# The shared product of the first spectral layer: added on VectorE, or copied by ScalarE into the bank that TensorE then adds onto

## The chip, the cores and the metric

The kernel runs on one core of one Trainium2 chip. The metric is the device time of one execution in microseconds (us). TensorE (PE) multiplies, with its weight loads shown apart as PEld; VectorE (DVE) and ScalarE (ACT) do the elementwise work; GpSimd (POOL) does a little of it; the DMA queues are fed mostly by SyncE (SP). PSUM, where the products land, has eight banks of 512 fp32 values in each of 128 partitions.

## The reference, cut to what matters

```
Xf = rfft2(x)                                   # x: [2, 1, 4096, 640], over the 4096 positions
z  = Xf in 4 blocks of 160 channels;  zr, zi
hr = relu(zr @ w1[0] - zi @ w1[1] + b1[0])      # layer 1, per block
hi = relu(zi @ w1[0] + zr @ w1[1] + b1[1])
or_ = hr @ w2[0] - hi @ w2[1] + b2[0]           # layer 2
oi_ = hi @ w2[0] + hr @ w2[1] + b2[1]
a  = irfft2(softshrink(or_) + 1j * softshrink(oi_))
b  = (gelu(x @ w_gate) * (x @ w_up)) @ w_down
out = sigmoid(sum(x * gate_w)) * a + (1 - gate) * b
```

The change lies in the first two lines of `h`. The two complex sums hold one product in common: with s = zr + zi, each of hr and hi is a product of s with one matrix, plus a product of one part of z with another matrix. The kernel works out three products in place of four.

## The kernel before, in words

All products run as pairs of fp32r parts: an operand is split into a rounded high part, written by ScalarE (`high`, L285), and the rest, written by VectorE or GpSimd (`low`, L288). A product is then three matmuls, high by high, high by low and low by high (`mms`, L305 to L307).

The kernel has three stretches. To about 1360 us run the gate and up projections and the first step of the forward transform. From about 1360 to 1760 us run the two spectral layers. After that run the last step of the inverse transform and the down projection.

The spectral stretch is a list of 64 steps (b, c, n): two batch entries, eight chunks of 256 frequencies, four blocks of channels. Chunk (0, 0) is wider by two columns ("wide") and takes a path of its own; it is steps 4 to 7. The program order of each engine is the order in which the Python code issues instructions, and each engine keeps to it. One pass i of the loop over the steps issues:

- in some passes `rest`, the second transform step for the channels that the blocks leave over: a transform on TensorE, then `high` and `low` of `zz`. It stands ahead of layer 1;
- `main_z` for step i+1: eight matmul records of the transform (`fwd2`, L993), then on ScalarE the high part `z` and a copy `zt` (L1005), on VectorE the low part of `z` and the sum `zt` (L1008). What is left, the split of `zs` (that is s), is returned as a function `sums`;
- `mlp1` for step i: the shared product `pk` (3 matmuls on `zs`); `kc`, its copy to SBUF by ScalarE (L1096); two groups of 5 matmuls, one for each half of the bank `pm`; two VectorE additions of `kc` onto them, `hs` (L1103); `sums()`; `relu_split` of `hs` into `h` (ScalarE L1056, VectorE L1057); then the 32 channels left over, `last` (5 matmuls, L1079 to L1081), with a ScalarE copy (L1109) and a VectorE sum (L1110);
- `mlp2` for step i-1: two times 8 matmuls on `h`, each followed by a ScalarE activation `m` (L1138) and a VectorE instruction `y` (L1139);
- `more()`: two ScalarE activations `hl` (L1113, L1114) and one VectorE instruction (L1115) for step i;
- where i is odd, `inv1` for the pair that ended at step i-2: 12 matmuls, two copies `is` on ScalarE (L1174) and two on VectorE (L1176);
- where i is even, `y_split` for the pair that ended at step i-1: two `high` of `ys` on ScalarE, one `low` on VectorE and one on GpSimd.

So ScalarE's queue at the start of a pass holds, for odd i, the two `ys` of the pass before, then `zz` if there is a `rest`, then `z`, `zt` and `kc`. For even i it holds the two `is` instead of `ys`.

The banks of PSUM come from one pool of eight. A bank goes back when the last instruction that reads it is through.

Of the kernel before, what the change touches and what calls it, by code (L numbers as in the profile page):

```python
# [12 lines left out]
AF = mybir.ActivationFunctionType  # L13
OP = mybir.AluOpType

P = 128
# [6 lines left out]
CH = 256  # L23
# [198 lines left out]
def spectral_mix_kernel(ctx: ExitStack, tc: tile.TileContext, a):  # L222
    nc = tc.nc
# [11 lines left out]
    def bank():  # L235
        return psum.tile([P, 512], F32, name="bank", tag="bank")
# [6 lines left out]
    def mid(shape, dt=F32, name="mid"):  # L243
        if not gap:
            gap.extend([tiny([P, 1], name="gap"), pool.tile([P, 112], F32, name="gap", tag="gap", bufs=1)])
            for t in gap:
                nc.gpsimd.memset(t, 0.0)
        return pool.tile(shape, dt, name=name, tag="mid", bufs=14)

    def small(shape, dt=F32, name="small"):  # L250
        return pool.tile(shape, dt, name=name, tag="small", bufs=18)

    def tiny(shape, dt=F32, name="tiny"):
        return pool.tile(shape, dt, name=name, tag="tiny", bufs=15)
# [7 lines left out]
    def flush():  # L262
        for dst, src in late:
            ld(dst, src)
        late.clear()
# [12 lines left out]
    b1r = consts.tile([64, NBLK], F32, name="b1r")  # L278
# [16 lines left out]
    def by_two(m):  # L295
        return m.rearrange("p (k i) -> p i k", k=2)

    def mm3(dst, pairs):

        ops = []  # L300
        for (lh, ll), (rh, rl) in pairs:
            ops += [(lh, rh)] + ([(ll, rh)] if ll is not None else []) + [(lh, rl)]
        mms(dst, ops)

    def mms(dst, ops):  # L305
        for i, (l, r) in enumerate(ops):
            nc.tensor.matmul(dst, l, by_two(r), start=i == 0, stop=i == len(ops) - 1)  # L307

# [622 lines left out]
    wide = lambda b, c: (b, c) == (0, 0)  # L933
# [6 lines left out]
    def two(b, c, name):  # L940

        if wide(b, c):
            return [mid([P, 2, CW], F32R, name=name) for h in range(2)]
        t = mid([P, 2, 2, CH], F32R, name=name)
        return [t[:, h] for h in range(2)]
# [3 lines left out]
    def part_of(b, c, k):  # L949

        if not wide(b, c):
            return tiny([P, CH], name=("zt", "kc", "hs")[k])
        if not WT:
            WT.append(mid([P, 3, CW], name="wt"))
        return WT[0][:, k]
# [28 lines left out]
    def sc_pop(b, c):  # L984
        for b_, kp in [(b, kp) for kp in range(4)] + ([(1, 0)] if wide(b, c) else []):
            SC.pop((b_, c, kp))
# [53 lines left out]
    def main_z(b, c, n):  # L1040
        F = width(b, c)
        z = two(b, c, "z")
        if wide(b, c):
            zs = small([P, 2, F], F32R, name="zs")
            zs = [zs[:, h] for h in range(2)]
        else:
            if chunks.index((b, c)) < 2 * NCH - 4:
                zs = mid([P, 2, F], F32R, name="zs")
                zs = [zs[:, h] for h in range(2)]
            else:  # L1050
                zs = [tiny([P, F], F32R, name="zs") for h in range(2)]
        Z[b, c, n] = z, zs
        return fwd2(b, c, P * n, z, zs)

    def relu_split(dh, dl, src):
        nc.scalar.activation(dh, src, AF.Relu)  # L1056
        nc.vector.scalar_tensor_tensor(dl, src, 0.0, dh.bitcast(F32), op0=OP.max, op1=OP.subtract)  # L1057

    def mlp1(b, c, n, sums):
        F = width(b, c)  # L1060
        z, (sh, sl) = Z.pop((b, c, n))
        w, wl = W1[n], W1L[n]
        t1, t2 = ZL1[b, c], ZL2[b, c]

        part = lambda k: (w[:, k:k + P], w[:, LOW1 + k:LOW1 + k + P])
        wl = wl.rearrange("p h c -> p (h c)")


        def group(dst, m):
            r = 1 - m  # L1070
            wh, wlo = part(OUT1[m])
            mms(dst, [(wh, z[0][:, r]), (wh, z[1][:, r]), (wlo, z[0][:, r]),
                      (wl[:, P * m:P * m + P], t1[:, n, :F]), (wl[:t2.shape[0], 384 + P * m:512 + P * m], t2[:, n, :F])])

        def last(dst):

            for r in range(2):
                k = LAST1[r]
                nc.tensor.matmul(dst, w[:, k:k + P], by_two(z[0][:, r, :F]), start=r == 0, stop=False, skip_group_check=True)  # L1079
                nc.tensor.matmul(dst, w[:, k:k + P], by_two(z[1][:, r, :F]), start=False, stop=False, skip_group_check=True)  # L1080
            nc.tensor.matmul(dst, wl[:, 256:384], by_two(t1[:, n, :F]), start=False, stop=True, skip_group_check=True)  # L1081
        h = two(b, c, "h")
        if wide(b, c):
            if n < 2:
                x = small([P, 2, CW], F32R, name="hl")
                nc.gpsimd.memset(x[64:66, 1].bitcast(F32), 1.0)
                HW[n] = x[:, 0], x[:66, 1]
            hA, hB = HW[n % 2]
        else:
            hA, hB = hl1[n % 2], hl2[n % 2]  # L1090
        H[b, c, n] = (h, hA, hB)
        pk = bank()
        wh, wlo = part(OUT1["k"])
        mms(pk[:, :F], [(wh, sh[:, :F]), (wh, sl[:, :F]), (wlo, sh[:, :F])])
        kc, hs = part_of(b, c, 1), (small if wide(b, c) else mid)([P, 2, F], name="hs")
        nc.scalar.activation(kc[:, :F], pk[:, :F], AF.Copy)  # L1096
        pm = [bank()] * 2 if F == CH else [bank(), bank()]
        for r in range(2):
            d = pm[r][:, r * CH:(r + 1) * CH] if F == CH else pm[r][:, :F]
            group(d, r)  # L1100
        for r in range(2):
            d = pm[r][:, r * CH:(r + 1) * CH] if F == CH else pm[r][:, :F]
            nc.vector.tensor_add(hs[:, r, :F], d, kc[:, :F])  # L1103
        sums()
        relu_split(h[0], h[1], hs)
        pl = bank()
        last(pl[:, :F])
        hs = part_of(b, c, 2)[:64]
        nc.scalar.activation(hs, pl[64:, :F], AF.Copy)  # L1109
        nc.vector.scalar_tensor_tensor(hs, pl[:64, :F], b1r[:, n:n + 1], hs, op0=OP.add, op1=OP.add)  # L1110

        def rest_of():
            nc.scalar.activation(hB[:64, :F], hs, AF.Relu)  # L1113
            nc.scalar.activation(hA[:64, :F], hs, AF.Relu)  # L1114
            nc.vector.scalar_tensor_tensor(hA[64:, :F], hs, 0.0, hB[:64, :F].bitcast(F32), op0=OP.max,  # L1115
                                           op1=OP.subtract)
        return rest_of
# [229 lines left out]
    def h_s4(i):  # L1347
        d = HR[i]
        for k in range(2):
            nc.vector.tensor_sub(d["s2"][k], d["a12"][k], d["s2"][k])  # L1350
        d["s4"] = d.pop("s2")
# [163 lines left out]
    last = len(keys) - 1  # L1515
# [59 lines left out]
    for k, (b, n2) in enumerate(a_seq):  # L1575
        i, j = steps_a[k]
# [16 lines left out]
    for i, (gr, tp) in enumerate(keys):  # L1593
        if deep((gr, tp)) and tp % 2:
            p, f = x_deep(gr, tp)
# [9 lines left out]
    for k, (l, pb) in enumerate(((1, 0), (1, 1), (2, 0), (2, 1))):  # L1605
        s0 = (5, 12, 19, 26)[k]
        f = prep(l, pb)
# [15 lines left out]
    for i, key in enumerate(keys):  # L1623
# [18 lines left out]
        for j, t in enumerate(quads):  # L1642
# [10 lines left out]
            n = len(late)  # L1653
# [18 lines left out]
    steps = [(b, c, n) for b, c in chunks for n in range(NBLK)]  # L1672
    S = len(steps)
    steps[S - 6:S - 2] = [(1, NCH - 1, 0), (1, NCH - 1, 1), (1, NCH - 2, 2), (1, NCH - 2, 3)]
    uu, ahead = {}, {}
    todo = {}
    for ch in range(1, 2 * NCH):
        b, c = chunks[ch]
# [6 lines left out]
    def events(i, j):  # L1685
        for f, *args in todo.get((i, j), []):
            f(*args)
    wl = lambda part, *js: [(wd_load, j, part) for j in js]
# [13 lines left out]
    for i in range(S + 2):  # L1702
        events(i, 0)
        flush()
        if i < S:
            events(i, 1)
            if i + 1 < S:
                sums = main_z(*steps[i + 1]) if i else ahead_z
                if steps[i + 1][2] == 3:
                    sc_pop(*steps[i + 1][:2])  # L1710
            more = mlp1(*steps[i], sums if i + 1 < S else lambda: None)
        if 0 <= i - 1 < S:
            mlp2(*steps[i - 1])
        if i < S:
            more()
        if 0 <= i - 2 < S and steps[i - 2][2] % 2:
            inv1(steps[i - 2][0], steps[i - 2][1], steps[i - 2][2] // 2)
            if wide(*steps[i - 2][:2]) and steps[i - 2][2] == 3:
                HW.clear()
                WT.clear()  # L1720
        if 0 <= i - 1 < S:
            b, c, n = steps[i - 1]
            if n % 2:
                y_split(b, c, n // 2)
            if i == S:
                uu.update(inv2(0))
        for f, *args in fin.get(i, []):
            f(*args)


    SEQ = dict(enumerate(("s3", "s4", "a12", "a22", "s1")))
    DUO = {0: "s1", 2: "s3", 3: "a12", 4: "s4"}
    for i in range(len(c_seq)):
        n = i + 1 if i + 1 < len(c_seq) else None
# [3 lines left out]
        def step(k):  # L1738
            def f():
# [7 lines left out]
                if k == (1 if i else 0):  # L1747
                    h_s4(i)
                op = (SEQ if i == 0 else DUO).get(k)
                if op:  # L1750
# [44 lines left out]
```

## Time and profile before

| | |
|---|---|
| median of 3 runs | 2466.82 us (2465.4 to 2467.61) |
| the profiled execution | 2466.74 us |
| its span, first to last instruction | 2465.0 us |
| PE busy | 2445.0 us, 20239 matmuls |
| DVE busy | 2065.8 us |
| ACT busy | 1486.9 us |
| POOL busy | 390.5 us |
| granted TensorE clock | 1.0 |
| DMA | 499.50 MB, 203 GB/s |

The busy time of an engine is the sum of its instructions' times, overlaps counted once. In a timeline each row is one instruction or a few alike in a row: start, time, engine, line, operation, out<-in, shapes, count, and in square brackets how long the engine had been idle before and what ended that. Matmuls are pipelined, so the rows of PE overlap: the start of the next row says more than the time of one.

### The profile page before, as it was taken

The page shows a single profiled execution, that of the slowest core. Times are in us where ns is not written, and L with a number is a line of the kernel's source. Part 1 is how long each engine was busy: PE and PEld are TensorE (multiplying, and loading weights), DVE is VectorE, ACT ScalarE, POOL GpSimd, SP SyncE. Part 2 cuts the span into 40 slices and gives each one's busy share as a digit, 9 for nine tenths or more (in the row PEclk, how much of TensorE's full clock was granted, in tenths as well). Part 3 has the DMA queues.
Part 4 walks back from the last instruction along what each step waited for, and adds up shares of the span by engine and source line. Part 5 has one row for each costly group of instructions (what it writes and reads, how often), then busy time and mean ns, then how long its engine had stood idle before and what let it go on. Part 6 is the DMA issues. An engine that isn't in the chain of part 4 may idle for free.

```text
span 2465.0 us, 54653 instructions
## 1 busy us (share of the span) xinstructions
PE 2445.0 (99%) x20239; PEld 2430.0 (99%) x20239; DVE 2065.8 (84%) x4323; ACT 1486.9 (60%) x3503; POOL 390.5 (16%) x404
## 2 busy tenths in 40 slices
PE   9999999999999999999999999999999999999999
PEld 9999999999999999999999999999999999999999
DVE  7777788777777877877767888888899999999998
ACT  5555556666666666666556788888744454455443
POOL 0111100000000000000003111111043334333342
PEclk9999999999999999999999999999999999999999
DMA  6666667777778687777677446467854444544443
GB/s 208 212 229 214 242 208 232 224 263 236 250 236 261 196 257 250 237 227 248 222 234 234 148 139 174 147 173 244 308 176 145 140 150 156 167 161 153 148 145 112
DMA packets 351422, 499.50 MB, mean 203 GB/s; under 512 B 26028, under 2 KB 223276, under 8 KB 351156
## 3 DMA queue, kind: packets, MB, share of 16 engines
q1 hardware_dynamic: 333684, 445.02, 56.1%
q0 software_dynamic: 17472, 51.00, 5.7%
q8 instruction: 159, 2.61, 0.4%
q14 instruction: 107, 0.88, 0.1%
HBM read 307.10 MB, written 188.81 MB: 201 GB/s over the span
## 4 chain that ended last, share of the span: by engine, by line
PE 71%; DVE 19%; issue 5%; DMA 3%; ACT 2%; SPq 0%; DVEq 0%; ACTq 0%
PE bank L572 48%; PE bank L307 11%; DVE ho L288 7%; PE bank L1421 6%; DVE s2s L288 3%; PE bank L993 3%; DVE uu L1426 2%; PE bank L704 2%; DVE uu L1389 1%; PE bank L827 1%; DVE hs L1350 1%; DMA s<-scr 1%; PE bank L1079 0%; PE bank L1080 0%; DMA xraw<-in_xT_dram 0%
## 5 line engine op out<-in xcount | busy, mean ns | idle before, releaser
L572 PE MATMUL bank<-xo,w 128*128 128x256 f32 x11196 | 1298.3, 275 | 3.1 <-ACT u L598 1.5
L572 PEld LDWEIGHTS bank<-xo,w 128*128 128x128 f32 x11196 | 1276.1, 192 | 5.9 <-ACT u L598 2.1
L1421 PE MATMUL bank<-wx,ho 128*128 128x320 f32 x3844 | 532.4, 300 | 5.6 <-DVE ho L288 5.5
L1421 PEld LDWEIGHTS bank<-wx,ho 128*128 128x128 f32 x3844 | 524.4, 189 | 10.2 <-DVE ho L288 10.0
L285 ACT ACTIVATE ho<-hraw 128x640 fp32r<-128x640 f32 x320 | 168.3, 574 | 118.5 <-PE bank L1421 83.7
L288 DVE TENSOR_TENSOR ho<-hraw,ho 128x640 fp32r<-128x640 f32 (+3 forms) x384 | 226.8, 632 | 6.4 <-ACT ho L285 3.4
L598 ACT ACTIVATE u<-bank 128x256 f32<-128x256 f32 x328 | 125.4, 382 | 161.2 <-PE bank L572 154.7
L288 DVE TENSOR_TENSOR xs<-xr,xs 64x640 fp32r<-64x640 f32 x128 | 105.0, 820 | 75.9 <-ACT xs L285 73.4
L650 DVE TENSOR_TENSOR u<-bank,u 128x256 f32<-128x256 f32 x204 | 85.9, 421 | 79.8 <-ACT u L598 78.7
L288 DVE TENSOR_TENSOR xo<-xraw,xo 128x512 fp32r<-128x512 f32 x194 | 133.3, 688 | 17.0 <-ACT xo L285 15.7
L307 PE MATMUL bank<-wm,h 128*128 128x320 f32 (+1 forms) x792 | 129.7, 300 | 0.5 <-DVE h L1057 0.4
L829 DVE TENSOR_TENSOR as<-bank,as 64x320 f32<-64x320 f32 x256 | 113.9, 484 | 18.3 <-ACT as L828 16.4
L285 ACT ACTIVATE xo<-xraw 128x512 fp32r<-128x512 f32 x194 | 121.7, 627 | 8.4 <-DMA xraw<-in_xT_dram 7.3
L598 ACT ACTIVATE p<-bank 128x256 f32<-128x256 f32 x144 | 55.3, 384 | 104.6 <-DVE h L661 57.7
L288 DVE TENSOR_TENSOR s2s<-s,s2s 128x320 fp32r<-128x320 f32 x128 | 115.7, 963 | 2.4 <-ACT s2s L285 1.5
L307 PEld LDWEIGHTS bank<-wm,h 128*128 128x128 f32 (+1 forms) x792 | 111.8, 186 | 2.1 <-DVE h L1057 0.6
L572 PE MATMUL bank<-wx,ho 128*128 128x320 f32 x764 | 110.4, 300 | 0.9 <-DVE ho L288 0.9
L285 ACT ACTIVATE xs<-xr 64x640 fp32r<-64x640 f32 x128 | 93.9, 734 | 28.2 <-DMA xr<-in_x_dram 26.4
L828 ACT ACTIVATE as<-bank 64x320 f32<-64x320 f32 x256 | 96.9, 427 | 20.3 <-PE bank L827 15.4
L572 PEld LDWEIGHTS bank<-wx,ho 128*128 128x128 f32 x764 | 105.7, 189 | 2.1 <-DVE ho L288 2.1
L780 POOL MEMSET h<- 64x512 f32 x16 | 8.3, 522 | 614.2 <-DVE h L665 178.2
L599 ACT ACTIVATE h<-bank 128x256 f32<-128x256 f32 x204 | 77.8, 381 | 29.4 <-PE bank L572 27.8
(196 smaller groups left out, 3892.8 us busy)
## 6 DMA issues: line engine op xcount, KB each, us to landing
xo<-xD SPq DMA_DIRECT2D x124, 512.0 KB
xraw<-in_xT_dram SPq DMA_DIRECT2D x215, 256.0 KB
hD<-h SPq DMA_DIRECT2D x184, 256.0 KB
hraw<-hD SPq DMA_DIRECT2D x128, 320.0 KB
xD<-xo POOLq DMA_DIRECT2D x64, 512.0 KB, 3.6
sc<-scr SPq DMA_DIRECT2D x65, 320.0 KB
xr<-in_x_dram SPq DMA_DIRECT2D x64, 320.0 KB
scr<-as SPq DMA_DIRECT2D x64, 320.0 KB
```

The costliest lines, as they stand in the source:

```text
L285: nc.scalar.activation(dst, src, AF.Copy, scale=scale)
L288: eng.tensor_sub(dst, src, hi.bitcast(F32))
L307: nc.tensor.matmul(dst, l, by_two(r), start=i == 0, stop=i == len(ops) - 1)
L572: nc.tensor.matmul(dst, l, by_two(r), start=first and i == 0, stop=i == len(ops) - 1, skip_group_check=True)
L598: copy = lambda d, s_: nc.scalar.activation(d, s_, AF.Copy)
L599: gelu = lambda d, s_: nc.scalar.activation(d, s_, AF.Gelu_apprx_tanh)
L650: nc.vector.tensor_add(u4, C, u4)
L704: nc.tensor.matmul(acc, l, by_two(r), start=first and i == 0, stop=i == 2, skip_group_check=True)
L828: nc.scalar.activation(stg[hi, cs], pa[lo, :320], AF.Copy)
L829: nc.vector.tensor_add(stg[hi, cs], pa[hi, :320], stg[hi, cs])
L993: nc.tensor.matmul(pz.rearrange("p (r e k f) -> p k r e f", r=2, e=2, k=4)[:, kp], SC[b, c, kp][:, o:o + P], ft.rearrange("p (r e f) -> p ...
L1421: nc.tensor.matmul((X, Y)[k], l, by_two(r), start=n[k] == 0 and not (more and k), stop=n[k] == tot[k] - 1, skip_group_check=True)
```

## The change: what it does, and the diff

For all steps but the wide ones:

- Two PSUM banks are taken at the first step and kept to the end of the stretch (`seeds`). They are used in turn. Each is written once at the start by a matmul over all its 512 columns with `start=True`.
- `pk` comes first in the step. ScalarE then copies it, read twice over, into both halves of the step's bank `d`: one instruction with 512 output columns into PSUM, in place of `kc` with 256 into SBUF.
- Behind that come `main_z` of step i+1 (`ahead()`), then `last`, then the two groups of 5 matmuls, now with `start=False`: they add onto what ScalarE wrote.
- The two VectorE additions `hs` are gone. `relu_split` reads the bank itself.
- `rest_sum`, the copy and sum for `last`, stands ahead of `sums()` and `relu_split`.

In the wide steps only the place of `ahead()` changes: it comes behind `pk`.

```
-    def mms(dst, ops):
+    def mms(dst, ops, first=True):
         for i, (l, r) in enumerate(ops):
-            nc.tensor.matmul(dst, l, by_two(r), start=i == 0, stop=i == len(ops) - 1)
+            nc.tensor.matmul(dst, l, by_two(r), start=first and i == 0, stop=i == len(ops) - 1, skip_group_check=not first)
...
+    seeds = []
+
-    def mlp1(b, c, n, sums):
+    def mlp1(b, c, n, ahead):
...
-                      (wl[:, P * m:P * m + P], t1[:, n, :F]), (wl[:t2.shape[0], 384 + P * m:512 + P * m], t2[:, n, :F])])
+                      (wl[:, P * m:P * m + P], t1[:, n, :F]), (wl[:t2.shape[0], 384 + P * m:512 + P * m], t2[:, n, :F])],
+                F > CH)
...
+        def rest_sum(pl):
+            hs = part_of(b, c, 2)[:64]
+            nc.scalar.activation(hs, pl[64:, :F], AF.Copy)
+            nc.vector.scalar_tensor_tensor(hs, pl[:64, :F], b1r[:, n:n + 1], hs, op0=OP.add, op1=OP.add)
+            return hs
...
-        kc, hs = part_of(b, c, 1), (small if wide(b, c) else mid)([P, 2, F], name="hs")
-        nc.scalar.activation(kc[:, :F], pk[:, :F], AF.Copy)
-        pm = [bank()] * 2 if F == CH else [bank(), bank()]
-        for r in range(2):
-            d = pm[r][:, r * CH:(r + 1) * CH] if F == CH else pm[r][:, :F]
-            group(d, r)
-        for r in range(2):
-            d = pm[r][:, r * CH:(r + 1) * CH] if F == CH else pm[r][:, :F]
-            nc.vector.tensor_add(hs[:, r, :F], d, kc[:, :F])
-        sums()
-        relu_split(h[0], h[1], hs)
-        pl = bank()
-        last(pl[:, :F])
-        hs = part_of(b, c, 2)[:64]
-        nc.scalar.activation(hs, pl[64:, :F], AF.Copy)
-        nc.vector.scalar_tensor_tensor(hs, pl[:64, :F], b1r[:, n:n + 1], hs, op0=OP.add, op1=OP.add)
+        if F == CH:
+            if not seeds:
+                seeds.extend(bank() for k in range(2))
+                for d in seeds:
+                    nc.tensor.matmul(d, wl[:, :P], t1[:, :2], start=True, stop=True)
+            pm = seeds.pop(0)
+            seeds.append(pm)
+            d = pm.rearrange("p (r f) -> p r f", r=2)
+            nc.scalar.activation(d, pk[:, None, :F].broadcast_to((P, 2, F)), AF.Copy)
+            sums = ahead()
+            pl = bank()
+            last(pl[:, :F])
+            for r in range(2):
+                group(d[:, r], r)
+            hs = rest_sum(pl)
+            sums()
+            relu_split(h[0], h[1], d)
+        else:
+            sums = ahead()
...
-            if i + 1 < S:
+            def following(i=i):
+                if i + 1 == S:
+                    return lambda: None
                 sums = main_z(*steps[i + 1]) if i else ahead_z
                 if steps[i + 1][2] == 3:
                     sc_pop(*steps[i + 1][:2])
-            more = mlp1(*steps[i], sums if i + 1 < S else lambda: None)
+                return sums
+            more = mlp1(*steps[i], following)
```

More of the change, by code (lines that the diff above doesn't have):

```diff
@@ L1094, in mlp1 @@
         mms(pk[:, :F], [(wh, sh[:, :F]), (wh, sl[:, :F]), (wlo, sh[:, :F])])
-        kc, hs = part_of(b, c, 1), (small if wide(b, c) else mid)([P, 2, F], name="hs")
-        nc.scalar.activation(kc[:, :F], pk[:, :F], AF.Copy)
-        pm = [bank()] * 2 if F == CH else [bank(), bank()]
-        for r in range(2):
-            d = pm[r][:, r * CH:(r + 1) * CH] if F == CH else pm[r][:, :F]
-            group(d, r)
-        for r in range(2):
-            d = pm[r][:, r * CH:(r + 1) * CH] if F == CH else pm[r][:, :F]
-            nc.vector.tensor_add(hs[:, r, :F], d, kc[:, :F])
-        sums()
-        relu_split(h[0], h[1], hs)
-        pl = bank()
-        last(pl[:, :F])
-        hs = part_of(b, c, 2)[:64]
-        nc.scalar.activation(hs, pl[64:, :F], AF.Copy)
-        nc.vector.scalar_tensor_tensor(hs, pl[:64, :F], b1r[:, n:n + 1], hs, op0=OP.add, op1=OP.add)
+        if F == CH:
[17 more added lines that the diff above has]
+            sums = ahead()
+            kc, hs = part_of(b, c, 1), small([P, 2, F], name="hs")
+            nc.scalar.activation(kc[:, :F], pk[:, :F], AF.Copy)
+            pm = [bank(), bank()]
+            for r in range(2):
+                group(pm[r][:, :F], r)
+            for r in range(2):
+                nc.vector.tensor_add(hs[:, r, :F], pm[r][:, :F], kc[:, :F])
+            sums()
+            relu_split(h[0], h[1], hs)
+            pl = bank()
+            last(pl[:, :F])
+            hs = rest_sum(pl)
         def rest_of():
@@ L1728, in spectral_mix_kernel @@
             f(*args)
+    seeds.clear()
     SEQ = dict(enumerate(("s3", "s4", "a12", "a22", "s1")))
```

## The prediction, on record before the changed kernel ran

> **What bounds the kernel now.** I read the page first, then the busy time by stretches, the waits of the spectral stretch, and its timeline, TensorE and ScalarE apart.
>
> ```profile
> span 2465.0 us, 54653 instructions
> ...
> PE 2445.0 (99%) x20239; PEld 2430.0 (99%) x20239; DVE 2065.8 (84%) x4323; ACT 1486.9 (60%) x3503; POOL 390.5 (16%) x404
> ```
>
> TensorE is busy for all but 20 us. An edit gains only where TensorE idles, or where it takes work from TensorE; it loses wherever it makes TensorE wait. The change keeps every matmul, so the second question is where TensorE idles in the stretch it touches.
>
> ```profile
> core 0: us, PE busy (x) PEld busy (x) DVE busy (x) ACT busy (x) POOL busy (x), PEclk, DMA share, GB/s
> 1412.00:1717.00 305.00, 305.00 (x2478) 303.58 (x2478) 263.36 (x577) 247.97 (x598) 38.01 (x25) 1.00 0.59 175
> 1717.00:1760.00 43.00, 41.20 (x321) 40.02 (x320) 35.60 (x77) 32.89 (x79) 5.24 (x5) 1.00 0.73 241
> 1760.00:1800.00 40.00, 36.71 (x262) 35.45 (x261) 37.39 (x69) 24.68 (x55) 9.70 (x8) 1.00 0.82 311
> ```
>
> In the steady part (steps 8 to 56) TensorE idles for 0.00 of 305 us at full clock. Only the last steps and what follows them show idle time, 1.8 and 3.3 us. VectorE (86% busy) and ScalarE (81%) are close behind, and where ScalarE idles it waits for VectorE:
>
> ```profile
> ACT zs L285 <- DVE zt L1008: 39.5, 47, 0.9
> ...
> ACT h L1056 <- DVE hs L1103: 11.2, 49, 0.3
> ```
>
> These 51 us are slack of ScalarE that TensorE never feels. The change spends it, and the point is where in the step it spends it.
>
> **Removed and lengthened work.** Grouped rows of the same window:
>
> ```profile
> L1103 DVE TENSOR_TENSOR hs<-bank,kc 128x256 f32<-128x256 f32 x98 | 36.6, 415 | 0.0
> ...
> L285 ACT ACTIVATE ys<-y 128x640 fp32r<-128x640 f32 x48 | 32.6, 730 | 0.0
> L1056 ACT ACTIVATE h<-hs 128x512 fp32r<-128x512 f32 x49 | 30.9, 631 | 11.2 <-DVE hs L1103 11.2
> L285 ACT ACTIVATE z<-bank 128x512 fp32r<-128x512 f32 x49 | 28.8, 587 | 0.3 <-PE bank L993 0.3
> ...
> L1096 ACT ACTIVATE kc<-bank 128x256 f32<-128x256 f32 x49 | 18.6, 380 | 0.0
> ...
> L285 ACT ACTIVATE zz<-bank 128x512 fp32r<-128x512 f32 x13 | 7.6, 581 | 0.0
> ```
>
> VectorE loses two `hs` a step, 36.6 us in these 49 steps. TensorE waits for nothing of VectorE's here (0.00 idle), so this counts nothing. ScalarE's copy grows from 256 columns into SBUF to 512 into PSUM. No row writes PSUM from ScalarE. The bounds are 0.38 us (`kc`, as if the second half were free) and 0.73 us (`ys`, more columns, SBUF on both sides). I take 0.59, from `z`: PSUM source and as many columns. The Trainium skill ("ScalarE: Activation LUTs", "Step-by-step: what each stage is for") says that PSUM is the lower-latency destination for ScalarE. If that were worth what the source's side shows here, 0.631 against 0.587 or 0.044 us, the sum below would be about 1.2 us smaller. No row here shows it. `relu_split` reading PSUM rather than SBUF differs by the same 0.04 us and is on no path of TensorE. The two first matmuls into the kept banks, 512 columns each, are once 0.4 us.
>
> **The added wait.** Until now nothing on TensorE waited for `kc`; only VectorE did. Now both groups wait for ScalarE's copy, the seed. Queued behind them on TensorE are `mlp2` of the step before and, in odd passes, `inv1`; ScalarE's `m` and VectorE's `y` wait for those in turn. So I ask when TensorE arrives at the groups, and when the seed is there. TensorE around an odd pass (step 39):
>
> ```profile
> 1604.00 0.43 PE L307 MATMUL bank<-wl,hl 128*128 128x320 f32 x2
> 1604.27 1.05 PE L993 MATMUL bank<-f,sc 128*128 128x128 f32 x8
> 1605.08 0.58 PE L307 MATMUL bank<-zs,wm 128*128 128x256 f32 x3
> 1605.49 0.50 PE L307 MATMUL bank<-z,wm 128*128 128x256 f32 x3
> ...
> 1606.61 0.28 PE L1079 MATMUL bank<-z,wm 128*128 128x256 f32 x1
> ...
> 1607.17 0.30 PE L307 MATMUL bank<-wm,h 128*128 128x320 f32 x1
> ```
>
> Call E the end of the previous pass's `mlp2`, 1604.27. From the starts of the rows, the transform takes 0.81 us, `pk` 0.41, `last` 0.56. In the new order `pk`, transform and `last` stand between E and the groups: TensorE arrives at E + 1.78. ScalarE over the same time:
>
> ```profile
> 1604.05 0.95 ACT L1138 ACTIVATE m<-bank,neg2lam 128x320 f32<-128x320 f32 x2
> 1604.90 0.41 ACT L1113 ACTIVATE hl<-hs 64x256 fp32r<-64x256 f32 x1
> 1605.20 0.41 ACT L1114 ACTIVATE hl<-hs 64x256 fp32r<-64x256 f32 x1
> 1605.51 1.36 ACT L285 ACTIVATE ys<-y 128x640 fp32r<-128x640 f32 x2
> 1606.76 0.58 ACT L285 ACTIVATE z<-bank 128x512 fp32r<-128x512 f32 x1
> ```
>
> The second `m` needs the last product of `mlp2`, which lands at 1604.00 + 0.43 = 1604.43; it starts at 1604.05 + 0.95 - 0.525 = 1604.48. So ScalarE has no lag here: it runs as early as TensorE lets it. Then come two `hl` and two `ys`, and it is free at 1606.76, E + 2.49. The change moves none of these; all stand ahead of the seed in ScalarE's queue. The seed therefore runs from E + 2.49 to E + 3.08. What a waiting TensorE loses besides:
>
> ```profile
> 1737.22 0.47 DVE L1110 SCALAR_TENSOR_TENSOR hs<-bank,b1r,hs 64x256 f32<-64x256 f32 x1
> ...
> 1737.74 0.60 PE L307 MATMUL bank<-zs,wm 128*128 128x256 f32 x3 [0.68 <-DVE hs L1110]
> 1738.18 0.56 PE L307 MATMUL bank<-z,wm 128*128 128x256 f32 x3
> ```
>
> From the releaser's end (1737.69) to the matmul are 0.05 us, and the two rows after it are 0.02 and 0.06 longer than those of step 39. So an odd step stalls for 3.08 + 0.05 - 1.78 + 0.08 = 1.43 us.
>
> In odd passes with a `rest`, both engines have more ahead of the groups:
>
> ```profile
> 1604.43 0.89 PE bank L993 x8
> 1616.22 1.78 PE bank L993 x16
> ```
>
> ```profile
> 1618.95 0.58 ACT L285 ACTIVATE zz<-bank 128x512 fp32r<-128x512 f32 x1
> 1619.43 0.59 ACT L285 ACTIVATE z<-bank 128x512 fp32r<-128x512 f32 x1
> ```
>
> The first two are of the chain of waits: TensorE has 1.78 - 0.89 = 0.89 us more, ScalarE 0.48 more. The stall is 1.43 - 0.89 + 0.48 = 1.02 us.
>
> Even passes have two `is` in place of `ys` ahead of the seed (step 38, TensorE's row and then ScalarE's):
>
> ```profile
> 1600.00 0.58 PE L307 MATMUL bank<-zs,wm 128*128 128x256 f32 x3
> ```
>
> ```profile
> 1599.75 0.74 ACT L1174 ACTIVATE is<-bank 128x320 f32<-128x320 f32 x2
> 1600.38 0.59 ACT L285 ACTIVATE z<-bank 128x512 fp32r<-128x512 f32 x1
> ```
>
> ScalarE is free 0.38 us after `pk` starts, before `pk` lands at 0.58. The seed then ends at 0.58 + 0.05 + 0.59 = 1.22; TensorE arrives at 0.41 + 0.89 + 0.56 = 1.86. No stall, 0.64 us to spare.
>
> **What else moves.** `z` and `zt` of the next step come behind the seed, 0.5 us later; `zs` is first needed one whole step on. `main_z` issues no DMA, so no queue of SP or POOL is passed. Two of eight banks are held for good; `pk`, the transform and `last` give theirs back within a step, so I count nothing, and price it below.
>
> **The sum.** Steps 9 to 55 hold 24 odd passes (48 `ys`), 13 with `zz`: 11 x 1.43 + 13 x 1.02 = 29.0 us. Steps 57, 59, 61 add 4.3. Step 63 has no transform to follow, so TensorE arrives at E + 0.97: 2.2. Step 3 is like one with `rest`: 1.0. The first matmuls: 0.4. Together 36.9. Given back: the 1.8 us idle of the last steps, and half of the 3.3 behind them, as waits that came from ScalarE and VectorE lagging; 3.4. Net +33.5 on the profiled run's 2466.74 (which is the median of 2466.82 but for 0.08): 2500.
>
> **The rivals.**
> *ScalarE ahead of TensorE (the other side).* The seed would have to start by E + 1.1, 1.4 us earlier than the rows allow, for instance because the freed VectorE lets ScalarE run ahead. For it: 51 us of waits on VectorE, part of which vanish. Against it: the second `m` is bound to TensorE's own product. If it came so, the gain is what TensorE idles, at most 1.8 + 3.3 = 5.1 us: 2461.7. It decides in the 24 odd passes. Chance 0.06 of faster; 0.05 that the seed is hidden and the idle time stays, 2467.
>
> *ScalarE stays behind.* In other passes of before it lags more:
>
> ```profile
> 1479.96 0.89 PE bank L993 x8
> ```
>
> ```profile
> 1483.10 0.58 ACT L285 ACTIVATE z<-bank 128x512 fp32r<-128x512 f32 x1
> ```
>
> Step 19: 3.14 us from the chain's transform to `z`, against 1606.76 - 1604.43 = 2.33 in step 39. If that 0.81 lasted, or if six banks made TensorE wait as much, 28 odd steps would cost 23 us more: 2523. Against it: each stall lets ScalarE catch up, which TensorE's steady stream does not. Chance 0.10.
>
> *The seed is cheaper or partly hidden,* so that half the stall remains: 2483. The seed would have to be there 0.7 us sooner, more than its whole 0.59, so this needs a second reason. Chance 0.06.
>
> *The change doesn't do what it says:* if matmuls overwrote the seed, the instructions and waits would be the same, and so the time.
>
> **How the numbers follow.** 0.73 for the forecast. The seed's bounds give 28 x (-0.21 to +0.14), -6 to +4 us, the end of the stretch some 3 either way: 2491 to 2507 for this case alone. Reaching to the cheaper case and half way to the dearer one gives 2483 to 2515, which leaves out the first rival's 0.11 and about half of the second's 0.10. About 0.2% (4.9 us) is what a measurement can tell from no change. Faster 0.06, same 0.05, slower 0.89.
>
> **What would show it.** In the changed profile, waits of the groups for ScalarE's seed, some 28, of 0.9 to 1.4 us, all in odd passes; the spectral stretch some 33 us longer with TensorE no longer fully busy; no such wait in even passes; the seed near 0.59 us. Wrong would be: waits in even passes too (lag or banks), no waits at all, or the seed well off 0.59.

## The result, and the profile after

The changed kernel takes 2498.86 us (median of 4 runs, 2497.56 to 2499.04) against 2467.05 us for the kernel before in the same runs: a ratio of 1.0129, 95% interval 1.0111 to 1.0146. It is slower by 32 us. The prediction said 2500.

The first lines of the page of the changed kernel:

```profile
span 2497.1 us, 54416 instructions
...
PE 2449.1 (98%) x20241; PEld 2431.0 (97%) x20241; DVE 2034.9 (81%) x4203; ACT 1504.1 (60%) x3503; POOL 390.1 (16%) x404
```

VectorE lost 30.9 us of work and ScalarE gained 17.2. TensorE's busy time grew by 4.1 us and the span by 32.1: TensorE waits. Busy time by stretches, columns as before:

```profile
1412.00:1717.00 305.00, 282.44 (x2262) 277.83 (x2261) 219.09 (x439) 241.31 (x549) 34.74 (x23) 1.00 0.52 153
```

In the window where TensorE idled for 0.00 us it now idles for 22.6. All instructions of ScalarE's copy, L1111 in the changed kernel, with those who waited for it (us in total, times; PEld is the same wait as the weight loads see it):

```profile
L1111 ACT ACTIVATE bank<-bank x60: 570/582/592, 1359.2 to 1787.5; 128x512 f32<-128x512 f32 x60
...
who waited for it (us, times):
  PEld bank L307: 37.3, 29
  PE bank L307: 31.7, 29
```

Of 60 seeds (ScalarE's copies of `pk` into the bank), 29 made TensorE wait. All are in odd passes: the 24 from step 9 to 55, and steps 3, 57, 59, 61 and 63. The timeline of one of them (TensorE, then ScalarE):

```profile
1432.63 0.50 PE L307 MATMUL bank<-zs,wm 128*128 128x256 f32 x3
...
1434.30 0.28 PE L1084 MATMUL bank<-zl,wl 128*128 128x256 f32 x1
...
1435.75 0.60 PE L307 MATMUL bank<-z,wm 128*128 128x256 f32 x3 [1.18 <-ACT bank L1111]
1436.19 0.39 PE L307 MATMUL bank<-zl,wl 128*128 128x256 f32 x2
```

```profile
1432.83 0.53 ACT L1161 ACTIVATE m<-bank,neg2lam 128x320 f32<-128x320 f32 x1 [0.43 <-PE bank L307]
...
1433.25 0.40 ACT L1136 ACTIVATE hl<-hs 64x256 fp32r<-64x256 f32 x1
...
1433.56 0.40 ACT L1137 ACTIVATE hl<-hs 64x256 fp32r<-64x256 f32 x1
...
1433.87 1.35 ACT L285 ACTIVATE ys<-y 128x640 fp32r<-128x640 f32 x2
...
1435.12 0.58 ACT L1111 ACTIVATE bank<-bank 128x512 f32<-128x512 f32 x1
```

`pk` starts at 1432.63, right behind `mlp2`; that is E. TensorE is through with `last` and could start the groups at E + 1.78 (1434.30 + 0.11). The seed starts at 1435.12, E + 2.49, behind `m`, two `hl` and two `ys`, and the groups start at 1435.75. The square bracket says 1.18 because the row of the last matmul lasts 0.28 us, and the next one could have started 0.11 us behind its start; the wait is 1.34, 0.16 more than the bracket. The three matmuls that follow take 0.44 us to the next row where 0.33 is usual.

ScalarE's own waits changed too. In the window from 1412 to 1717 of the changed kernel:

```profile
ACT zs L285 <- DVE zt L1008: 30.7, 45, 0.7
...
ACT m L1161 <- PE bank L307: 15.5, 41, 0.5
```

Before, ScalarE waited for TensorE almost never. Now its `m` waits for `mlp2` in 41 passes: in these ScalarE has caught up with TensorE, so that no lag of its own adds to the stalls.

### The profile page after: what moved, and what is told of

Same layout as the page of the kernel before. It is cut to its first block, busy times and chain, and to the rows that moved or that the text cites. A ratio compares the mean times of both kernels' runs of the same rounds, so it can differ in the third digit from the quotient of the medians.

```text
span 2497.1 us, 54416 instructions
## 1 busy us (share of the span) xinstructions
PE 2449.1 (98%) x20241; PEld 2431.0 (97%) x20241; DVE 2034.9 (81%) x4203; ACT 1504.1 (60%) x3503; POOL 390.1 (16%) x404
## 5 line engine op out<-in xcount | busy, mean ns | idle before, releaser
L288 DVE TENSOR_TENSOR ho<-hraw,ho 128x640 fp32r<-128x640 f32 (+3 forms) x384 | 219.9, 615 | 7.2 <-ACT ho L285 4.2
L288 DVE TENSOR_TENSOR s2s<-s,s2s 128x320 fp32r<-128x320 f32 x128 | 124.6, 1032 | 1.3 <-ACT s2s L285 0.3
L307 PE MATMUL bank<-z,wm 128*128 128x256 f32 (+1 forms) x384 | 67.9, 286 | 31.7 <-ACT bank L1111 31.7
```

The costliest lines, as they stand in the source:

```text
L288: eng.tensor_sub(dst, src, hi.bitcast(F32))
L307: nc.tensor.matmul(dst, l, by_two(r), start=first and i == 0, stop=i == len(ops) - 1, skip_group_check=not first)
```

## The experiments

The theory: the seed is late because ScalarE's queue holds `hl`, `hl`, `ys` and `ys` ahead of it, and these stand behind an `m` that cannot start before `mlp2` ends. The rivals: ScalarE is too loaded as a whole; two banks fewer are too few; the later transform is what costs. Each run is compared with runs of the kernel before on the same chip, whose median was 2463.0 to 2465.67 us. The edits are against the changed kernel, or the run that a heading refers to.

### The changed kernel again

> The changed kernel once more, to stand beside the other runs on this chip. Every theory expects the ratio to before that it had, 1.011 to 1.015, and waits of 1.34 and 0.93 us in odd passes.

2500.41 us, ratio 1.0141 (1.0124 to 1.0157), with the same 29 waits, 31.7 us in total.

### The ys copies behind the seed

The loop over `pend` stands in `following`, behind `main_z` of step i+1.

```
+                for f in pend:
+                    f()
+                pend.clear()
...
-                y_split(b, c, n // 2)
+                if i + 1 < S:
+                    pend.append(lambda b=b, c=c, n=n: y_split(b, c, n // 2))
+                else:
+                    y_split(b, c, n // 2)
```

> The two ys copies of an even pass are issued in the next pass, behind the seed, z and zt; all else is as in the changed kernel. Theory (the seed is late because it is queued behind hl, hl, ys, ys): ScalarE is free for the seed at E + 1.24 in place of E + 2.49, the seed is there at E + 1.88, TensorE arrives at E + 1.78. The odd stalls shrink to 0.1 to 0.2 us without a rest and vanish with one, and the time is 2463 to 2470 us. Rival (ScalarE lags as a whole, or six banks are too few): the waits stay or move to another place in the pass, and the time stays above 2485.

2473.03 us, ratio 1.0037 (1.0023 to 1.0050). The waits for the seed are all but gone from the steady part (in steps 57, 59 and 63 the weight loads still wait 0.7 to 1.0 us), and the ratio falls from 1.0141 to 1.0037. That is the theory's place and not the rival's, but the time is 3 us above the range. TensorE's waits from 1412 to 1717 us of this run, the longest:

```profile
PEld bank L307 <- DVE y L1162: 5.3, 21, 0.3
...
PEld bank L307 <- ACT bank L1111: 0.5, 3, 0.2
```

Behind nearly every odd pass (21 of 24) the next `pk` waits for a bank whose last reader, `y`, is late on VectorE. What made VectorE late stands ahead of `y` in its queue: the instructions that write `zs`, in this run and then in the changed kernel.

```profile
L288 DVE TENSOR_TENSOR zs<-zt,zs x48: 424/898/1386, 1414.4 to 1715.3; 128x256 fp32r<-128x256 f32 x48
```

```profile
L288 DVE TENSOR_TENSOR zs<-zt,zs x45: 424/425/426, 1415.2 to 1715.4; 128x256 fp32r<-128x256 f32 x45
```

The same instruction takes up to 1.386 us where it took 0.425. 24 of the 48 are long, and all 24 lie beside GpSimd's part of `ys`, the short ones never. One of them:

```profile
1447.28 1.87 POOL L288 TENSOR_TENSOR ys<-y,ys 128x640 fp32r<-128x640 f32 x1 [11.10 <-ACT ys L285]
...
1448.05 1.38 DVE L288 TENSOR_TENSOR zs<-zt,zs 128x256 fp32r<-128x256 f32 x1
```

### The same, with no work on GpSimd

```
             split(t[:, 0], t[:, 1], y.rearrange("p r m q n -> p r (m q n)"),
-                  nc.gpsimd if j == 1 and (b, c, pb) < (1, NCH - 2, 1) else nc.vector)
+                  nc.vector)
```

> The run with the ys copies behind the seed, and both low parts of ys on VectorE, none on GpSimd. In that run VectorE's low part of zs took 1.386 us at most and 0.424 at least, the long ones while GpSimd worked on ys. Theory (the two engines hinder each other on SBUF): all of them take 0.42 us now. VectorE then has 0.82 us more of ys ahead of zs in its queue, so pk waits for zs about as before, and the time stays within 0.2% of that run (ratio 1.002 to 1.006). Rival (the long ones wait for something in ScalarE or the stores): some still take over 1 us.

2466.90 us, ratio 1.0008 (0.9998 to 1.0017): no change from the kernel before. All `zs` are short:

```profile
L288 DVE TENSOR_TENSOR zs<-zt,zs x49: 402/425/427, 1413.6 to 1715.6; 128x256 fp32r<-128x256 f32 x49
```

The durations are as the theory said; that the time would stay was wrong. I had taken the wait at `pk` for one on `zs`, and reckoned that VectorE's 0.82 us of extra `ys` would delay `zs` by as much as GpSimd had. It was a wait for the bank that `y` frees. It is gone, and the ratio fell from 1.0037 to 1.0008, which is 7 us. So the whole loss of the change can be undone by the place of two ScalarE copies and the engine of one subtraction.

### The hl activations behind the seed

`following` has the loop over `pend` here too.

```
-            more()
+            if i + 1 < S and not wide(*steps[i][:2]) and not wide(*steps[i + 1][:2]):
+                pend.append(more)
+            else:
+                more()
```

> The two hl activations (and their VectorE instruction) of a step are issued in the next pass behind the seed, z and zt; the ys copies stay ahead of it. Theory: the seed comes 0.61 us sooner in each of 28 odd passes, the waits fall from 1.34 and 0.93 to about 0.73 and 0.32, and the time falls by 17 us to 2479 to 2485. Rival (lag as a whole): moving 0.61 us within ScalarE's queue changes nothing, 2495 to 2502.

2500.80 us, ratio 1.0152 (1.0138 to 1.0166): no gain. The theory's 2479 to 2485 us was missed, and the time is where the rival put it. But the trace does not bear the rival out. TensorE's rows in an odd pass:

```profile
1465.97 0.60 PE L307 MATMUL bank<-z,wm 128*128 128x256 f32 x3 [0.61 <-ACT bank L1111]
...
1467.19 0.98 PE L307 MATMUL bank<-wm,h 128*128 128x320 f32 x6
...
1468.36 0.51 PE L307 MATMUL bank<-wl,hl 128*128 128x320 f32 x2 [0.19 <-DVE hl L1138]
```

The wait for the seed fell from 1.18 to 0.61, by 0.57 of the 0.61 expected. Most of it came back in the first half of `mlp2`, at the two matmuls that read `hl`: VectorE's part of `hl` now stands behind `z` and `zt`, which stand behind the seed. The first of them starts 0.35 us late (1467.19 + 0.82 is 1468.01; it starts at 1468.36). Even passes, where nothing had been late, became 0.3 us longer at the same place. My expectation had no row for that.

### The seed written twice

```
             nc.scalar.activation(d, pk[:, None, :F].broadcast_to((P, 2, F)), AF.Copy)
+            nc.scalar.activation(d, pk[:, None, :F].broadcast_to((P, 2, F)), AF.Copy)
```

> The seed is written twice, one copy behind the other. Theory: 0.48 us more on the path of 29 odd passes, and within the 0.64 us to spare of the even ones: 13 to 14 us more, 2510 to 2514, waits of 1.8 and 1.4 us in odd passes alone. Rival (ScalarE's total work is the bound): all 60 steps pay, 27 us more, 2524 to 2528.

2520.87 us, ratio 1.0236 (1.0221 to 1.0252). Against the changed kernel run again, on another chip, that is 23 us more by the ratios and 19.2 more by the spans of the two profiled runs (2517.8 and 2498.6 us). Both lie between the theory's 13 to 14 and the rival's 27, so the time alone does not decide; the trace does. ScalarE in an odd pass with a `rest`, and who waited for the second copy in the whole run:

```profile
1451.33 0.58 ACT L285 ACTIVATE zz<-bank 128x512 fp32r<-128x512 f32 x1
1451.81 0.58 ACT L1111 ACTIVATE bank<-bank 128x512 f32<-128x512 f32 x1
1452.42 0.58 ACT L1112 ACTIVATE bank<-bank 128x512 f32<-128x512 f32 x1
```

```profile
  PE bank L307: 49.5, 32
```

32 waits, not 60: the even passes kept clear but for three. The second copy cost 0.61 us, not 0.48: in the trace it waits for a semaphore that the first raises at its end (1451.81 + 0.58), while `zz` and the first copy overlap. 29 x 0.61 is 17.7. The theory had the place right and the price too low. The clock also halved twice in this run, as the last section shows.

### The new order with the old sum

```
-            nc.scalar.activation(d, pk[:, None, :F].broadcast_to((P, 2, F)), AF.Copy)
+            kc, hm = part_of(b, c, 1), mid([P, 2, F], name="hs")
+            nc.scalar.activation(kc[:, :F], pk[:, :F], AF.Copy)
             sums = ahead()
...
+            for r in range(2):
+                nc.vector.tensor_add(hm[:, r], d[:, r], kc[:, :F])
             sums()
-            relu_split(h[0], h[1], d)
+            relu_split(h[0], h[1], hm)
```

Here `d` is an ordinary bank and the groups start afresh.

> The new order of the step (pk, transform, last, groups) with the old arithmetic: ScalarE copies pk to SBUF (256 columns), VectorE adds it twice, the groups start afresh and wait for no one. Theory (the loss is the groups' wait for the seed, not the order): no wait at the groups, ratio 1.000 to 1.004; zs is made 0.8 us later against its use than before, so some waits of pk on zs may grow. Rival (the later transform makes zs or z late, and that is what costs): ratio above 1.008.

2475.43 us, ratio 1.0037 (1.0024 to 1.0051): at the upper end of the theory's range, far from the changed kernel's 1.0141. The new order is not free, as 0.37% (9 us) is clear of the noise, but it is not the loss. TensorE's longest waits, all short:

```profile
PEld bank L307 <- DVE zs L288: 4.7, 9, 0.5
PEld bank L1082 <- DVE y L1159: 4.5, 20, 0.3
```

### The kernel before with six banks

```
+        if not held:
+            held.extend(bank() for k in range(2))
+            for d in held:
+                nc.tensor.matmul(d, wl[:, :P], t1[:, :2], start=True, stop=True)
...
+    for d in held:
+        nc.vector.tensor_copy(neg2lam, d[:, :1])
+    held.clear()
```

> The kernel before, with two of the eight banks taken through the spectral stretch and used for nothing (each is written once and one column of it is read at the end). Theory (banks are not short): ratio 0.998 to 1.002. Rival (two banks fewer make TensorE wait): ratio above 1.005, with new waits of TensorE for VectorE's last readers of banks.

2476.67 us, ratio 1.0047 (1.0033 to 1.0061). This misses the theory's range and comes out just under the rival's 1.005: two banks are worth about 11 us to the kernel before. TensorE waits in `inv1` of odd passes, which takes four banks in a row:

```profile
PEld bank L307 <- DVE hs L1116: 11.0, 22, 0.8
```

L1116 is the VectorE sum for `last`. I had counted the banks at nothing. In the changed kernel they cost nothing to be seen: TensorE's waits in that window are those for the seed. That could be because TensorE stands still in every odd pass while VectorE reads the banks empty. But the run above with no work on GpSimd and the one below with `m` in another pool hold the same two banks, have no stall at the seed, and show no such wait either. All three kernels lack VectorE's two additions. So the price of two banks is not a fixed one; that VectorE's relief takes it away was not tried by itself.

### The groups behind mlp2

`between` issues `mlp2` of step i-1.

```
             last(pl[:, :F])
-            for r in range(2):
-                group(d[:, r], r)
             hs = rest_sum(pl)
             sums()
+            between()
+            nc.scalar.activation(hB[:64, :F], hs, AF.Relu)
+            nc.scalar.activation(hA[:64, :F], hs, AF.Relu)
+            nc.vector.scalar_tensor_tensor(hA[64:, :F], hs, 0.0, hB[:64, :F].bitcast(F32), op0=OP.max, op1=OP.subtract)
+            for r in range(2):
+                group(d[:, r], r)
             relu_split(h[0], h[1], d)
```

> The two groups come behind mlp2 of the step before (16 matmuls, 2.18 us), and hl ahead of relu_split. Theory: TensorE arrives at the groups at E + 3.96, the seed is there at E + 3.13, no stall in any pass; what TensorE idled in the last steps of before goes too, and the time is 2460 to 2466, at or a little under before. Where it could go wrong: h of a step now has 1.86 us from the groups' end to mlp2, and needs 1.5. Rival (lag or banks): TensorE waits for h or a bank in place of the seed, above 2475.

2462.69 us, ratio 0.9997 (0.9988 to 1.0005): the loss is gone, as the theory said, and no wait for the seed is left. What TensorE still waits for lies in the last steps:

```profile
1712.52 0.53 ACT L1168 ACTIVATE m<-bank,neg2lam 128x320 f32<-128x320 f32 x1 [1.96 <-DMA scr<-is]
...
1714.19 0.40 PE L307 MATMUL bank<-wm,h 128*128 128x320 f32 x1 [0.96 <-ACT h L1056]
```

`m` waits for a buffer that a store of `is` still reads; `relu_split` is queued behind `m` on ScalarE, and TensorE needs its `h`.

### The same, with m in another pool

```
-            m = small([P, 320], name="m")
+            m = (small if wide(b, c) else mid)([P, 320], name="m")
```

> As the run with the groups behind mlp2, and m takes its buffer from the pool in which hs stood before the change, in place of the pool that it shares with the stored is. There, m waited 4.6 us for stores to end in the last steps, and relu_split, queued behind m on ScalarE, made TensorE wait 1.1, 0.6, 1.7 and 0.6 us. Theory: these four waits go, 4 us less than that run, ratio 0.997 to 0.9995. Rival: in that pool m waits for something else in the last steps (weights are loaded into it), and the ratio stays at 0.9990 to 1.001.

2458.99 us, ratio 0.9972 (0.9962 to 0.9983), inside the theory's range. This beats both kernels, the one before by 0.28%. Busy time in the two windows:

```profile
1412.00:1717.00 305.00, 305.00 (x2494) 304.58 (x2493) 238.93 (x483) 260.63 (x607) 40.08 (x27) 1.00 0.60 177
1717.00:1800.00 83.00, 81.71 (x623) 80.79 (x622) 74.07 (x141) 60.06 (x136) 16.77 (x14) 1.00 0.83 294
```

TensorE idles 1.3 us from 1717 to 1800, where it had idled 5.1 before. Whether the kernel before would gain from the moved buffer alone was not tried.

### The old sum in that place

```
-            nc.scalar.activation(d, pk[:, None, :F].broadcast_to((P, 2, F)), AF.Copy)
+            kc = part_of(b, c, 1)
+            nc.scalar.activation(kc[:, :F], pk[:, :F], AF.Copy)
...
+            for r in range(2):
+                nc.vector.tensor_add(hm[:, r], d[:, r], kc[:, :F])
-            relu_split(h[0], h[1], d)
+            relu_split(h[0], h[1], hm)
```

> As the last run (groups behind mlp2, m in the other pool), but with the old arithmetic: ScalarE copies pk to SBUF, VectorE adds it twice behind the groups, relu_split reads the sums. It asks what the seed is worth once TensorE no longer waits for it. Theory: the path from the groups' end to h grows by the two additions, some 0.75 us, to 2.2 us, against 1.86 us until the next mlp2 in the passes that have no inv1 between; TensorE waits some 0.4 to 0.6 us for h there, and the ratio to before is 1.002 to 1.007, against 0.997 with the seed. Rival (the place and the pool of m are the whole gain, the seed gives nothing): ratio 0.996 to 0.999, no waits for h.

2512.27 us, ratio 1.0201 (1.0186 to 1.0216): the theory's direction, at three times the upper end of its size.

```profile
ACT h L1056 <- DVE hs L1121: 52.1, 42, 1.3
...
PE bank L307 <- DVE h L1057: 13.1, 41, 0.3
...
PE bank L307 <- ACT h L1056: 8.7, 18, 0.7
```

I had added the two sums' own 0.75 us. They also stand in VectorE's queue behind the `y` of `mlp2` and `hl`, and nearly every pass pays. So this place, which makes the best kernel with the seed, is a bad one for the old sum as it is queued here; another place for the two additions was not tried. Once TensorE does not wait for the seed, the change is worth something: 0.28% against the kernel before.

## Why the prediction was right

**The bound.** Right. TensorE's steady stream was the bound, VectorE's relief gave nothing by itself, and TensorE's new waits cover the whole loss.

**The seed's length.** I took 0.59 us; it measures 0.582. The Trainium skill ("ScalarE: Activation LUTs", "Step-by-step: what each stage is for") calls PSUM ScalarE's lower-latency destination. This trace does not show it: from 1412 to 1717 us of the changed kernel the seed takes 0.581 us on average, and copies of as many columns from PSUM into SBUF take 0.578 (`zz`) and 0.589 (`z`). I had set 0.044 beside it as its price, and overlooked `zz`, which stood in my own list at 0.581.

**The stall of an odd pass.** E + 2.49, E + 1.78, 1.43 us: the profile after has E + 2.49, E + 1.78 and 1.34 + 0.11. A second reading takes the start of the last matmul of `mlp2` in every pass of both traces. In an odd pass the changed kernel falls behind by 1.44 to 1.50 us without a `rest` and by 0.99 to 1.09 with one (0.87 in step 53), where I had 1.43 and 1.02; steps 9, 59 and 63 stand apart and come below. The runs with `ys` moved, with the seed doubled and with the groups put later each moved this stall. That ScalarE's queue order sets it is shown, not argued.

**The even passes.** Right: none of them waited.

**The sum.** The waits are 31.7 + 29 x 0.16 = 36.3 us, with 0.10 each for the start that follows 39.2; I had 36.5 without the first matmuls. Two odd passes were dearer. In step 9 the bracket says 1.63 us, where other passes with a `rest` have 0.73 to 0.82: two ScalarE rows of 2x320 that the wide chunk adds, an `m` and a `ny`, stand ahead of the seed. In step 59 it says 2.44, as `m` of that pass came late. And behind step 63 the clock halved, which cost some 1.7 us and was no term of mine. Against that, some 7 us came back, where I had 3.4. By the same pass-by-pass reading 3.1 of them lie in the last steps and 1.8 right behind, nearly all of the old idle time there; I had counted half of what lay behind. Some 2 more lie in the steady part, where I had read 0.00 us of idle time: seven of its even passes had been 0.16 to 0.33 us longer before, too little at one place to show as idle time. So the stalls were right term by term, but that the total came within 2 us is in part luck: misses of about 4 us on either side cancelled.

**The rivals.** ScalarE's lag did not last, as its waits for TensorE show. The banks did matter to the kernel before, which I had put at nothing; in the changed kernel no wait for them is seen. The price of that rival, 23 us on top, was not seen.

## What to carry to other kernels

A cheaper sum is worth only what its place in the queues allows: before an instruction is put between two matmul groups, list what its engine's queue holds ahead of it at that moment and when the first of those can start. Here 30.9 us of work came off VectorE, for which TensorE had hardly waited, and gained nothing by itself. One ScalarE instruction a step, put on TensorE's path, cost 32 us, though ScalarE had 51 us of its own waits to spare. If a wait appears, look for matmuls that are ready and can stand ahead of it: here 16 of them hid the seed entirely, and with one buffer moved besides a loss of 1.4% became a gain of 0.3%.

## What the runs showed of the hardware

TensorE's clock fell after some stalls. In step 63 of the changed kernel TensorE idled 2.07 us by its row, and the matmuls that followed ran at half the clock for 3.4 us (0.50 from 1788.5 to 1791.8 us):

```profile
1788.00:1792.00 4.00, 3.82 (x17) 3.82 (x18) 1.73 (x3) 1.10 (x3) 2.35 (x2) 0.57 1.03 383
1792.00:1796.00 4.00, 4.00 (x32) 4.00 (x31) 2.44 (x6) 3.10 (x9) 0.00 (x0) 1.00 1.02 423
```

The granted clock is 0.57 on average in the first of these stretches and 1.00 in the next, and TensorE issued 17 matmuls in the first and 32 in the second. Half of 3.4 us, some 1.7 us, was lost here. The run with the doubled seed shows it twice (0.56 from 1424 to 1427 us, 0.57 from 1696 to 1700), each time about a microsecond behind the end of a stall whose bracket says 1.86 and 1.85 us. The length of a stall does not decide it. In this run of the changed kernel step 59 had a bracket of 2.44 us, and the clock stayed at 1.00. In the second run of the same kernel it fell behind step 59 (2.43; 0.50 from 1762.9 to 1766.2 us) and stayed at 1.00 behind step 63 (2.07). What decides was not tried.

A VectorE instruction of 128x256 with both sides in SBUF took up to 1.386 us in place of 0.425 while GpSimd worked on another tile, and 0.425 again when GpSimd's work was taken away. GpSimd's own instruction took 1.87 us there, against 1.55 in the changed kernel. VectorE's part of `z`, which reads a bank of PSUM, took 0.691 us in the changed kernel with GpSimd at work beside it and without. Why they hinder each other the runs do not show.
